# Products of a job under way go ahead of a due batch of values, and the second query block ends in two halves

## The chip, the core and the metric

The kernel runs on one core of a Trainium2 chip. The metric is device time in microseconds (us) of one execution. The kernel before was timed three times: 915.96, 916.36 and 916.58 us, median 916.36. A separate profiled execution took 916.05 us; its trace spans 914.0 us from the first to the last instruction.

## What is computed

A transformer layer with layer normalisation ahead of each part: attention with 32 heads of 20 columns over 2,048 rows of 640 columns, and then a gated product with 1,728 inner columns. Only the attention has an exponential; the gate is a plain product of two projections.

```
x = A_x                                            # 1 x 2048 x 640
qkv = layernorm(x) @ wqkv                          # 32 heads, 20 columns each
p = softmax(q @ k.T * 20 ** -0.5)                  # 2048 x 2048 for each head
h = x + (p @ v) @ wo
g = layernorm(h) @ w_gate;  u = layernorm(h) @ w_up
out = h + (g * u) @ w_down                         # 1728 inner columns
```

## The kernel before

**Blocks, groups, passes.** The 2,048 queries are cut into four blocks of 512 (b = 0 to 3), the 32 heads into eight groups of four. A pass handles one group with one block, against all 16 tiles of 128 keys. A pass named by a digit takes all 512 queries of its block; one named by a letter takes a half of 256 (`PASS`, lines 328 and 329): "C" and "D" are the halves of block 2, "A" and "B" those of block 3. Lines 330 to 339 write out the order of the passes. Blocks 0 and 1 run all eight groups in full; blocks 2 and 3 run `SPLIT_G` = 2 groups in full, then the other six for the first half and again for the second.

**Score tiles.** All passes together are cut into 683 score tiles of 1,536 columns (the last is shorter). For tile i, `emit_S` (line 519) puts the score products on PE (L533), which write one of two PSUM buffers `sc`; then ACT takes the exponential (L547) into one of six buffers `E`. In some tiles DVE takes the last 512 columns instead, by a polynomial in four steps (`emit_x`, lines 572 to 594: L580, L590, L591, L585); ACT's instruction is then 1,024 columns wide. Whether it does is decided by `x_takes` (line 566) for each tile: among its conditions, DVE must not be behind by the kernel's own bookkeeping, and in block 3 there must be `room()` (line 561), that is, the remaining tiles must leave room for the products of the tails that are still to be done.

**Values.** `emit_AV` (line 707) takes the finished exponentials in batches and multiplies them by the values (L740), accumulating in `acc`; a finished pass is copied out by DVE (L752) and divided by its sums. For most passes the division goes through DRAM: `norm` (line 629) sends the sums out and back (L636, L637), DVE takes reciprocals (L647), SP sends them to DRAM (L649) and back, spread over partitions (four transfers, L652), and DVE multiplies (L655). For the passes in `FAST` it is `job_norm` on PE.

**Jobs.** All other PE work is a queue of jobs: projections of q and k (L303), of values (L317), and the tail of each finished block, which is `job_out` (L978), normalisation, transposes (L283), the gate (`glu_sum` L1065 for 512 rows, `glu_two` L1083 for a half) and `job_y` (L1129, evacuated at L1133, stored by L1139). `run_job` (line 501) puts as many products of a job into each score tile's slot as fit by the bookkeeping `at` of expected times. Where nothing fits, `keep_warm` (L496) and line 529 put products with no use there. `due` (line 1306) lists the tails: a tail starts when its groups are normalised. The tails of blocks 0 and 1 take 512 rows, those of blocks 2 and 3 256. In the gate each of seven parts needs a pair of weight tiles (up and gate, 320 KB each), loaded by SP (L1036) into two buffers each. A program order by hand puts the spills of q to DRAM (L935, L936) behind block 0's tail. When the first tile of block 3 is reached, `load_res` puts four pairs for good into the buffers `qa`.

**The main loop** (lines 1310 to 1340) does this for each tile: scores and exponential; up to two batches of values; due events; a new tail if one is due; a job (`run_job`); fillers.

**The end.** After the last tile, `last_tail` (line 1218) does the last half of block 3 alone. It computes `out` for two row tiles (L1230, L1234), statistics on DVE, the scaled rows (DVE L1257, ACT L1258), then runs what is left in the queue of jobs (`fill`, line 1259), then transposes (lines 1260 and 1261), the gate (L1065) and `job_y`. What `fill` finds is `job_y` of the half before ("A"): one of its four pieces is held back for it by `add_tail` (lines 1190 to 1193), the others are there if they were not reached earlier.

Of the kernel before, what the change touches and what calls it, by code (L numbers as in the profile page):

```python
# [21 lines left out]
D = 640  # L22
H = 32
DH = 20
NT = S // P
# [3 lines left out]
HPG = 4  # L29
NG = H // HPG  # L30
VS = DH + 1
VW = H * VS + (SLOT - VS) + 1
QB = 512
# [6 lines left out]
FP = 7  # L40
FPW = 256
G1 = 4
SPLIT_G = 2
QA = 3 * QB
RES0 = 3
SM_SCALE = float(DH) ** -0.5
# [15 lines left out]
WO_NS, SUMS_NS, ROOT_NS, ROWS_NS = 1500, 6000, 5000, 5000  # L62
END_OF_TIME = 10 ** 9
WARM_LATE, NEXT_DVE = 0, 300
HOLD_AT, HOLD_NS = 5300, 450
AV_ROUNDS, X_LATE = 2, 0
FULL_IN, FULL_NS, ALL_NS = 2083, 300, 760
# [18 lines left out]
def kernel(  # L86
# [193 lines left out]
    def job_T(ln, dst, eng="dve", ps=None, after=None):  # L280
        ps = bank(BF16, D) if ps is None else ps
        for c in range(KT):
            nc.tensor.transpose(ps[:, c * P:(c + 1) * P], ln[:, c * P:(c + 1) * P], ident[:])  # L283
# [30 lines left out]
    def job_V(t, half):  # L314
        ps = bank()
        for c in range(KT):
# [9 lines left out]


    PASS = {"0": (0, 0, QB), "1": (1, 0, QB), "2": (2, 0, QB), "3": (3, 0, QB),
            "C": (2, 0, HW), "D": (2, HW, HW), "A": (3, 0, HW), "B": (3, HW, HW)}
    segs = []  # L330
    for ch in range(NB):
        for g in range(G1):
            kind = "copy" if ch == 0 else "last" if ch == NB - 1 else "add"
            segs.append(("0", g, ch * TPB, (ch + 1) * TPB, kind))
    segs += [("0", g, 0, NT, "only") for g in range(G1, NG)]
    segs += [("1", g, 0, NT, "only") for g in range(NG)]
    for full, halves in ("2", "CD"), ("3", "AB"):
        segs += [(full, g, 0, NT, "only") for g in range(SPLIT_G)]
        segs += [(p, g, 0, NT, "only") for p in halves for g in range(SPLIT_G, NG)]
    FINAL = len(segs) - 1  # L340
    TAILS = {0: [0], 1: [0], 2: [0, 2]}
    FAST = {("C", NG - 1), ("D", NG - 1), ("A", NG - 1), ("B", NG - 2)}

    tiles, cur_t, pos = [], [], 0
    for s, (p, g, lo, hi, _) in enumerate(segs):
# [358 lines left out]

    final = {}

    def emit_AV(upto):
        put_x()
        if not av_q:
# [274 lines left out]
            yield NEXT  # L984

    ln2 = {"open": 0, "rows": 0}
    COLUMNS_OF = {(1, 0): (0, 0), (1, 2): (0, 0), (2, 0): (1, 0), (2, 2): (1, 0), (3, 0): (2, 0)}

    def ln2_pieces(st, ts, key):
        while ln2["open"] >= 2 and not now["forced"]:  # L990
# [157 lines left out]
    LAST_B, LAST_T = NB - 1, [2, 3]  # L1148

    rows_in = set()  # L1150
    HELD_BY = {(1, 0): [(0, 0)], (2, 0): [(0, 2)], (2, 2): [(1, 0)], (3, 0): [(1, 2)]}

    def rows(b, ts):
        if b not in tail_st:
# [4 lines left out]

    def rows_early(b, ts):  # L1160
        key = b, ts[0]
        if key in HELD_BY and key not in rows_in and all(("y",) + k in done for k in HELD_BY[key]):
            rows(b, ts)

    def add_tail(b, ts):
# [48 lines left out]
    def run(gen):  # L1214
        for _ in gen:
            pass

    def last_tail():
# [36 lines left out]
        for hf in range(2):  # L1255
            cs = slice(hf * HALF, (hf + 1) * HALF)
            nc.vector.tensor_scalar(ls[ta][:, cs], ps_h[ta, hf][:, 0:HALF], m32[:, 0:1], r[:, 0:1], ALU.subtract, ALU.mult)  # L1257
            nc.scalar.activation(ls[tb][:, cs], ps_h[tb, hf][:, 0:HALF], ACT.Identity, bias=mr[:, 1:2], scale=r[:, 1:2])  # L1258
# [16 lines left out]
    def fill():  # L1275
        while step() is not None:
            pass
# [23 lines left out]
    def normed(p, gs):  # L1301
# [1 line left out]

    n_tiles = len(tiles)
    first_last = next(k for k, (us, _) in enumerate(tiles) if PASS[segs[us[0][0]][0]][0] == LAST_B)
    due = [("0", range(NG), 0, [0, 1, 2, 3]), ("1", range(NG), 1, [0, 1, 2, 3]), ("C", range(SPLIT_G, NG), 2, [0, 1]),
           ("D", range(SPLIT_G, NG), 2, [2, 3]), ("A", range(SPLIT_G, NG), 3, [0, 1])]
    PARTS = [d[2:] for d in due]
    i = 0
    while i < n_tiles or av_q:  # L1310
        now["i"] = i
        if i < n_tiles:
            emit_S(i)
        else:
            while step_x():
                pass
        if i == first_last:
            for g in range(NG):
                ensure(("spill", g))
            load_res()  # L1320
        if i == n_tiles:
            root = small.tile([P, 1], BF16, name="root")
            nc.scalar.activation(root[:], ones[:], ACT.Sqrt)
        for _ in range(2):
            emit_AV(i if i >= n_tiles else i - 2 if i >= LAG else i - 3)
            if not av_q or min(u[0] for u in av_q) > i - E_BUFS + 1:
                break
        run_events(i)
        if due:
            rows_early(*due[0][2:])  # L1330
        while due and normed(*due[0][0:2]) and (len(due[0][1]) == NG or normed(str(due[0][2]), range(SPLIT_G))):
# [112 lines left out]
```

## Time and profile before

| what | us |
|---|---|
| three timed runs | 915.96, 916.36, 916.58 |
| the profiled execution's own time | 916.05 |
| its span | 914.0 |
| ACT busy | 866.2 |
| PE busy | 817.5 |
| DVE busy | 702.1 |
| first exponential starts, last one ends | 15.6, 869.9 |

How to read it: each engine runs its own list of instructions in order, and semaphores hold one back until others are done. A row "x515 | 717.2, 1520 | 5.7" has the count, the time in which at least one of the group ran, the mean duration of one in ns (neighbours overlap), and the idle time of the engine ahead of them, with what ended it behind an arrow. In a timeline each row has its start and length. Rows of stretches have, for each engine, busy time and the count, then the granted clock of PE, the busy share of the DMA engines and GB/s.

### The profile page before, as it was taken

What the parts mean: (1) busy time and instruction counts of PE and PEld (TensorE: products, weight loads), DVE (VectorE), ACT (ScalarE), POOL (GpSimd) and SP (SyncE); (2) the same over time, 40 slices, a digit from 0 to 9 for tenths busy, and PEclk for the clock granted to TensorE, in tenths of its full rate; (3) what the DMA queues carried; (4) which work ended last, traced back from release to release, by engine and by line L of the source; (5) the groups of instructions that cost most, each with busy time, mean ns of one, the idle gap of its engine ahead of it and who ended that gap; (6) DMA issues with size and microseconds to landing.
All of it is one profiled execution on the core that took longest, in us unless ns stands there. A gap on an engine that the chain in (4) does not pass through costs nothing.

```text
span 914.0 us, 20094 instructions
## 1 busy us (share of the span) xinstructions
PE 817.5 (89%) x8035; PEld 346.8 (38%) x8115; DVE 702.1 (77%) x1310; ACT 866.2 (95%) x719; POOL 57.4 (6%) x255
## 2 busy tenths in 40 slices
PE   8788999889989899899897888999998999998897
PEld 5233333222223222233232333434434445444575
DVE  8664349899999899899998999798998784542243
ACT  6999999999999999999999999999999999999931
POOL 4210000000001200000003000020001000010000
PEclk9999999999999999999999999999999999999999
DMA  6000011011025022212410022021411211201310
GB/s 195 17 14 1 1 27 27 14 24 37 4 61 149 13 71 72 64 49 90 160 28 14 20 70 68 19 54 49 117 51 42 73 28 51 57 15 50 80 44 18
DMA packets 74203, 46.54 MB, mean 51 GB/s; under 512 B 20380, under 2 KB 70440, under 8 KB 74104
## 3 DMA queue, kind: packets, MB, share of 16 engines
q1 hardware_dynamic: 74104, 45.20, 18.0%
q8 instruction: 65, 1.06, 0.5%
q14 instruction: 34, 0.28, 0.1%
HBM read 37.88 MB, written 7.30 MB: 49 GB/s over the span
## 4 chain that ended last, share of the span: by engine, by line
ACT 67%; issue 17%; PE 10%; DVE 4%; DMA 1%; POOL 1%; SPq 0%; ACTq 0%
ACT E L547 67%; PE sc L533 2%; PE f L1065 2%; PE f L1129 2%; PE acc L740 1%; DVE st L201 1%; PE mi L303 1%; PE mi L978 0%; PE f L1230 0%; PE mi L496 0%; DMA wu<-in_B_w_up_dram 0%; PE mi L317 0%; PE mi L1083 0%; DVE kT L310 0%; DVE vx L270 0%
## 5 line engine op out<-in xcount | busy, mean ns | idle before, releaser
L547 ACT ACTIVATE E<-sc 128x1536 bf16<-128x1536 f32 (+1 forms) x683 | 848.7, 1417 | 6.2 <-PE sc L533 5.9
L533 PE MATMUL sc<-qa,kT 32*128 32x512 bf16 (+1 forms) x1920 | 203.2, 340 | 28.6 <-ACT E L547 16.9
L533 PEld LDWEIGHTS <-kT 32*128 32x128 bf16 x2816 | 84.1, 91 | 244.6 <-issue 206.1
L740 PE MATMUL acc<-E,vx 128*32 128x256 bf16 (+1 forms) x2592 | 170.3, 326 | 1.7 <-DVE vx L270 1.2
L580 DVE TENSOR_SCALAR xv<-sc 128x512 f32<-128x512 f32 x167 | 115.0, 689 | 30.2 <-PE sc L533 26.5
L585 DVE SCALAR_TENSOR_TENSOR xe<-xt,xv 128x512 int16<-128x512 f32 x167 | 113.3, 682 | 1.0
L591 DVE SCALAR_TENSOR_TENSOR xt<-xt,xv 128x512 f32<-128x512 f32 x167 | 112.3, 681 | 0.5
L590 DVE SCALAR_TENSOR_TENSOR xt<-xv 128x512 f32<-128x512 uint16 x167 | 112.0, 683 | 0.3
L303 PE MATMUL mi<-lnT,wp 128*128 128x512 bf16 x279 | 83.3, 381 | 11.7 <-DVE qa L310 5.5
L740 PEld LDWEIGHTS <-vx 128*32 128x32 bf16 x2816 | 55.8, 95 | 66.4 <-issue 63.8
L533 PE MATMUL sc<-qb,kT 32*128 32x256 bf16 (+1 forms) x896 | 68.2, 288 | 8.1 <-ACT E L547 5.3
L1129 PE MATMUL mi<-wd,hh 128*128 128x320 bf16 x336 | 58.2, 301 | 1.6 <-DVE xr L1133 1.6
L740 PE MATMUL acc<-xe,vx 128*32 128x512 bf16 (+1 forms) x224 | 50.6, 332 | 0.0
L1129 PEld LDWEIGHTS <-hh 128*128 128x128 bf16 x448 | 38.7, 97 | 30.6 <-issue 18.7
L303 PEld LDWEIGHTS <-wp 128*128 128x128 bf16 x310 | 25.0, 97 | 55.9 <-issue 44.3
L310 DVE TENSOR_SCALAR kT<-mi,one_row 128x512 bf16<-128x512 f32 x30 | 22.5, 750 | 28.1 <-PE mi L303 24.7
L1065 PE MATMUL mi<-ln2T,wg 128*128 128x512 bf16 x128 | 38.0, 382 | 5.8 <-DVE u L270 5.2
L496 PE MATMUL mi<-kT,ident 128*128 128x512 bf16 x116 | 37.8, 386 | 5.5 <-DVE ln2T L270 1.0
L978 PE MATMUL mi<-wo,on 128*128 128x320 bf16 x224 | 40.5, 301 | 2.2 <-DVE xr L982 2.0
L1065 PE MATMUL mi<-ln2T,wu 128*128 128x512 bf16 x128 | 37.3, 382 | 4.3 <-DVE hh L1073 3.5
L1083 PE MATMUL mi<-ln2T,qa 128*128 128x256 bf16 x240 | 34.6, 274 | 4.1 <-DVE hh L1091 3.0
L207 POOL CAST mb<-mv 128x2 bf16<-128x2 f32 (+1 forms) x10 | 2.3, 231 | 528.6 <-DVE mv L202 410.9
(143 smaller groups left out, 645.0 us busy)
## 6 DMA issues: line engine op xcount, KB each, us to landing
wu<-in_B_w_up_dram SPq DMA_DIRECT2D x23, 320.0 KB
wg<-in_B_w_gate_dram SPq DMA_DIRECT2D x23, 320.0 KB
bc<-scr SPq DMA_DIRECT2D x80, 64.0 KB
qsp<-qa SPq DMA_DIRECT2D x8, 384.0 KB
xr<-in_A_x_dram SPq DMA_DIRECT2D x16, 160.0 KB
bc<-scr SPq DMA_DIRECT2D x76, 32.0 KB
out_dram<-xr SPq DMA_DIRECT2D x14, 160.0 KB
wd<-in_B_w_down_dram SPq DMA_DIRECT2D x13, 160.0 KB
```

The lines of the kernel that those rows point to most:

```text
L303: nc.tensor.matmul(ps[:], lhsT=wslice(m, g, c), rhs=lnT[:, c, ch * QB:(ch + 1) * QB], start=(c == 0), stop=(c == KT - 1))
L496: nc.tensor.matmul(ps[:], lhsT=ident[:], rhs=kT[0][:, 0:BANK], start=True, stop=True)
L533: nc.tensor.matmul(sc[:, o:o + w], lhsT=kT[g][SLOT * j:SLOT * (j + 1), kt * P:(kt + 1) * P], rhs=q_of(g, b, c0, w)[SLOT * j:SLOT * (j + 1) ...
L547: exps = nc.scalar.activation(e[:, 0:n_act], sc[:, 0:n_act], ACT.Exp, bias=EXP_BIAS, scale=SM_SCALE)
L580: took = nc.vector.tensor_scalar(v[:], ps, X_SCALE, X_BASE, ALU.mult, ALU.max)
L585: nc.vector.scalar_tensor_tensor(e[:], t[:], X_R, v[:], ALU.mult, ALU.add)
L590: lambda: nc.vector.scalar_tensor_tensor(t[:], u, X_P, u, ALU.add, ALU.mult),
L591: lambda: nc.vector.scalar_tensor_tensor(t[:], t[:], X_Q, u, ALU.add, ALU.mult),
L740: nc.tensor.matmul(acc["t"][SLOT * j:SLOT * (j + 1), 0:w], lhsT=vx[kt][:, VS * h:VS * h + SLOT], rhs=e, start=(acc["n"][j] == 0), stop=(ac ...
L978: nc.tensor.matmul(ps[:, 0:HALF], lhsT=on[g][:, t * P:(t + 1) * P], rhs=wo[g][:, cs], start=(g == 0), stop=(g == NG - 1))
L1065: nc.tensor.matmul(ps[:, 0:n], lhsT=st["w", fp][k][:, c, f_cols(fp, f2)], rhs=st["ln2T"][:, c, c0:c0 + n], start=(c == 0), stop=(c == KT - 1))
L1129: nc.tensor.matmul(ps[:, 0:HALF], lhsT=st["hh"][f // 2][:, f % 2, t * P:(t + 1) * P], rhs=late["Wd"][f][:, cs], start=(f == 0), stop=(f == ...
```

## The change

Four things are altered.

1. `SPLIT_G` becomes a number for each block: 4 for block 1, 2 for block 2, 1 for block 3. So block 1 too ends in two halves ("E", "F") for its last four groups, its tail comes in two tails of 256 rows, and block 3 has one full group instead of two. The tables that depend on it (`TAILS`, `FAST`, `COLUMNS_OF`, `HELD_BY`, `due`) follow.
2. `job_ahead` is called in the main loop ahead of the batches of values. If a batch is due (`av_ns` gives its expected time) and a job is in the middle of a piece, it puts products of that job ahead of the batch, as far as both fit.
3. `rows_early` waits until the buffers of the tails are open, and may then load rows of block 1 early too.
4. In `last_tail`, `fill` is followed by products with no use, so many that both last `LN_NS` = 3,300 ns together.

```diff
-SPLIT_G = 2
+SPLIT_G = {"1": 4, "2": 2, "3": 1}
...
+LN_NS = 3300
...
+            "E": (1, 0, HW), "F": (1, HW, HW), "C": (2, 0, HW), "D": (2, HW, HW), "A": (3, 0, HW), "B": (3, HW, HW)}
...
-    segs += [("1", g, 0, NT, "only") for g in range(NG)]
-    for full, halves in ("2", "CD"), ("3", "AB"):
-        segs += [(full, g, 0, NT, "only") for g in range(SPLIT_G)]
-        segs += [(p, g, 0, NT, "only") for p in halves for g in range(SPLIT_G, NG)]
+    for full, halves in ("1", "EF"), ("2", "CD"), ("3", "AB"):
+        segs += [(full, g, 0, NT, "only") for g in range(SPLIT_G[full])]
+        segs += [(p, g, 0, NT, "only") for p in halves for g in range(SPLIT_G[full], NG)]
...
-    TAILS = {0: [0], 1: [0], 2: [0, 2]}
-    FAST = {("C", NG - 1), ("D", NG - 1), ("A", NG - 1), ("B", NG - 2)}
+    TAILS = {0: [0], 1: [0, 2], 2: [0, 2]}
+    FAST = {("E", NG - 1), ("F", NG - 1), ("C", NG - 1), ("D", NG - 1), ("A", NG - 1), ("B", NG - 2)}
...
+    def av_ns(upto):
+        if not av_q or acc["seg"] not in (None, av_q[0][1]):
+            return 0
+        s = av_q[0][1]
+        if acc["seg"] is None and at["pe"] < at["acc"] and now["i"] < acc["from"] and min(u[0] for u in av_q) > now["i"] - E_BUFS:
+            return 0
+        w = PASS[segs[s][0]][2]
+        most, rows = AV_ROUNDS * QB // w, [0] * HPG
+        for u in av_q:
+            if u[0] > upto or u[1] != s:
+                break
+            rows[u[3]] = min(rows[u[3]] + 1, most)
+        left = acc["left"] if acc["seg"] == s else END_OF_TIME
+        if sum(rows) < min(most * HPG, left) and min(u[0] for u in av_q) > upto - E_BUFS + 3:
+            return 0
+        return SWITCH + -(-sum(rows) // HPG) * (w * 5 // 12 + 4)
+
+    def job_ahead(upto):
+        ns = av_ns(upto)
+        if not ns:
+            return
+        until = max(at["exp"] - S_EXP - MARGIN, at["slot"][-2]) - ns
+        if not cur["fresh"]:
+            run_job(until)
...
-    COLUMNS_OF = {(1, 0): (0, 0), (1, 2): (0, 0), (2, 0): (1, 0), (2, 2): (1, 0), (3, 0): (2, 0)}
+    COLUMNS_OF = {(1, 0): (0, 0), (1, 2): (0, 0), (2, 0): (1, 0), (2, 2): (1, 2), (3, 0): (2, 0)}
...
-    HELD_BY = {(1, 0): [(0, 0)], (2, 0): [(0, 2)], (2, 2): [(1, 0)], (3, 0): [(1, 2)]}
+    HELD_BY = {(1, 0): [], (1, 2): [(0, 0)], (2, 0): [(0, 2)], (2, 2): [(1, 0)], (3, 0): [(1, 2)]}
...
-        if key in HELD_BY and key not in rows_in and all(("y",) + k in done for k in HELD_BY[key]):
+        if key in HELD_BY and key not in rows_in and ("open",) in done and all(("y",) + k in done for k in HELD_BY[key]):
...
+        begun = at["pe"]
         fill()
+        warm_ps = bank()
+        for _ in range(int((LN_NS - (at["pe"] - begun)) / 216)):
+            nc.tensor.matmul(warm_ps[:], lhsT=ident[:], rhs=kT[0][:, 0:BANK], start=True, stop=True)
...
-    due = [("0", range(NG), 0, [0, 1, 2, 3]), ("1", range(NG), 1, [0, 1, 2, 3]), ("C", range(SPLIT_G, NG), 2, [0, 1]),
-           ("D", range(SPLIT_G, NG), 2, [2, 3]), ("A", range(SPLIT_G, NG), 3, [0, 1])]
+    due = [("0", range(NG), 0, [0, 1, 2, 3]), ("E", range(SPLIT_G["1"], NG), 1, [0, 1]), ("F", range(SPLIT_G["1"], NG), 1, [2, 3]), ("C", range(SPLIT_G["2"], NG), 2, [0, 1]),
+           ("D", range(SPLIT_G["2"], NG), 2, [2, 3]), ("A", range(SPLIT_G["3"], NG), 3, [0, 1])]
...
+        if LAG <= i < n_tiles:
+            job_ahead(i - 2)
         for _ in range(2):
             emit_AV(i if i >= n_tiles else i - 2 if i >= LAG else i - 3)
```

More of the change, by code (lines that the diff above doesn't have):

```diff
@@ L328 @@
     PASS = {"0": (0, 0, QB), "1": (1, 0, QB), "2": (2, 0, QB), "3": (3, 0, QB),
-            "C": (2, 0, HW), "D": (2, HW, HW), "A": (3, 0, HW), "B": (3, HW, HW)}
+            "E": (1, 0, HW), "F": (1, HW, HW), "C": (2, 0, HW), "D": (2, HW, HW), "A": (3, 0, HW), "B": (3, HW, HW)}
     segs = []
@@ L1330 @@
             rows_early(*due[0][2:])
-        while due and normed(*due[0][0:2]) and (len(due[0][1]) == NG or normed(str(due[0][2]), range(SPLIT_G))):
+        while due and normed(*due[0][0:2]) and (len(due[0][1]) == NG or normed(str(due[0][2]), range(SPLIT_G[str(due[0][2])]))):
             add_tail(*due.pop(0)[2:])
```

## The prediction

> **What bounds the kernel now.** I read the page first, its busy shares and slices.
>
> ```profile
> span 914.0 us, 20094 instructions
> PE 817.5 (89%) x8035; PEld 346.8 (38%) x8115; DVE 702.1 (77%) x1310; ACT 866.2 (95%) x719; POOL 57.4 (6%) x255
> ...
> DVE  8664349899999899899998999798998784542243
> ACT  6999999999999999999999999999999999999931
> ```
>
> ACT is full from the second slice until the last two. PE and DVE are high too, but DVE thins out in the last ten slices. Next the groups of instructions, shapes kept apart, and three stretches.
>
> ```profile
> L547 ACT ACTIVATE E<-sc 128x1536 bf16<-128x1536 f32 x515 | 717.2, 1520 | 5.7 <-PE sc L533 5.5
> L547 ACT ACTIVATE E<-sc 128x1024 bf16<-128x1024 f32 x168 | 178.2, 1100 | 0.5 <-PE sc L533 0.5
> L580 DVE TENSOR_SCALAR xv<-sc 128x512 f32<-128x512 f32 x167 | 115.0, 689 | 30.2 <-PE sc L533 26.5
> L585 DVE SCALAR_TENSOR_TENSOR xe<-xt,xv 128x512 int16<-128x512 f32 x167 | 113.3, 682 | 1.0
> L1083 PE MATMUL mi<-ln2T,wu 128*128 128x256 bf16 x90 | 11.9, 273 | 2.0 <-DMA wu<-in_B_w_up_dram 1.0 <-DVE hh L1091 0.8 <-DMA sums_all<-sums 0.2
> L496 PE MATMUL mi<-kT,ident 128*128 128x512 bf16 x116 | 37.8, 386 | 5.5 <-DVE ln2T L270 1.0 <-DVE hh L1091 0.7 <-DVE vx L270 0.6
> ```
> ```profile
> 100.00:760.00 660.00, 596.05 (x5682) 225.40 (x5739) 579.57 (x1019) 659.10 (x542) 33.75 (x115) 1.00 0.19 53
> 760.00:870.00 110.00, 99.96 (x1367) 54.82 (x1373) 42.13 (x87) 109.14 (x84) 3.60 (x19) 1.00 0.17 46
> 870.00:914.00 44.00, 37.71 (x313) 29.57 (x312) 17.44 (x51) 9.86 (x24) 0.00 (x0) 0.97 0.11 32
> ```
>
> Until 870 us the exponentials set the time: ACT stood idle ahead of them for 5.7 + 0.5 = 6.2 us in all. So before 870 there are two ways to gain: fewer columns for ACT, or fewer of those 6.2 us. After 870 comes a chain of 44 us on PE, ACT and DVE, which the exponentials no longer touch; it gains separately.
>
> **The exponentials.** The instruction lists of the two built programs have 683 each. Before, 168 are 1,024 wide, after it 178: DVE takes ten more pieces of 512 columns. By the mean durations one is worth 1520 - 1100 = 420 ns, so 4.2 us. By busy time over count it is 717.2/515 - 178.2/168 = 1.393 - 1.061 = 0.33 us, so 3.3 us, the other end. The mean durations compare like with like, so I take **-4.2**. All ten lie past tile 600, and 84 of the 683 run from 760 us on (the count of ACT in the second stretch), so this is after about 760. DVE needs four steps for each, about 0.69 us each by its rows: 27.4 us. From 760 to 870 it is idle for 110.00 - 42.13 = 67.9 us, which is the cover; without it the ten would cost up to 27.4 us of waiting. The count is in the program, whatever the chip does.
>
> **Block 1 in halves.** Five groups (four of block 1, one of block 3) go at 256 instead of 512 columns: 320 more score products and 320 more value products, each half as wide, so the columns that PE streams stay equal. Three more normalisations pass through SP and two through PE; 38 of the products with no use (L496) go, seven more stand at line 529. 38 at 0.39 us at most are 14.7 us of PE time that cover these and the 42 products of L1129 that move forward (below, 42 x 0.14 = 5.9 us). **0** for PE; DVE's extra small copies lie in the same 67.9 us. The rows of block 1 come by the same transfers, only earlier, and nothing waits behind them but SP.
>
> **Weights.** Split tails read their weights once for each half: nine more pairs over SP. Before, one pair came late where the profile shows it:
>
> ```profile
> 752.18 0.32 SPq L649 DMA_DIRECT2D scr<-ri  x1
> 753.59 2.60 SPq L652 DMA_DIRECT2D bc<-scr  x4
> 756.23 0.42 SPq L1036 DMA_DIRECT2D wu<-in_B_w_up_dram  x1
> ```
> ```profile
> 759.73 1.27 PE L1083 MATMUL mi<-ln2T,wu 128*128 128x256 bf16 x10 [1.03 <-DMA wu<-in_B_w_up_dram]
> ```
> ```profile
> 761.44 9.68 ACT L547 ACTIVATE E<-sc 128x1536 bf16<-128x1536 f32 x7 [0.84 <-PE sc L533]
> ```
>
> SP issued the pair only after a normalisation's five transfers, the first use stood two tiles on, PE waited 1.03 us and ACT 0.84. In the new lists that place is gone (the pair there has four tiles), but in block 1's first half a pair again stands behind one L649 and four L652, one tile ahead of its use. A tile is 660/542 = 1.22 us. So the change of this term lies between -0.84 (no stall), and +1.2 (the same stall, one tile longer); uncovered by any tile it would be about 3.5 us from the issue at 756.23 to 759.73, that is +2.7. I take **+0.2**, the middle of the nearer two.
>
> **Spills.** Behind block 0's tail stand 16 transfers of q.
>
> ```profile
> L936 SPq DMA_DIRECT2D qsp<-qb x8: 432/451/563, 432.1 to 441.9; - x8
> ```
> ```profile
> 440.00:445.00 5.00, 4.04 (x35) 1.20 (x34) 3.56 (x7) 5.00 (x5) 0.00 (x0) 1.00 0.83 317
> ```
> ```profile
> 527.06 1.62 SPq L1036 DMA_DIRECT2D wu<-in_B_w_up_dram  x1
> ```
>
> They kept the DMA engines busy until about 440 + 0.83 x 5 = 444.2 us, and the next weights came at 527. In the new lists weights for block 1's first half follow right behind the last spill, four tiles (4.9 us) ahead of their use. From the last spill's issue, about 442, to the drain are 2.2 us, and 3.5 for the landing make 5.7: 0.8 late. Bounds 0 and 1.6 (up and gate both late), taken **+0.4**.
>
> **Products ahead of values.** The gain is in a place like this one, where a key projection's last products stood behind a batch of values.
>
> ```profile
> 52.12 0.62 PE L740 MATMUL acc<-E,vx 128*32 128x512 bf16 x8
> 52.67 0.60 PE L303 MATMUL mi<-lnT,wp 128*128 128x512 bf16 x2
> 53.31 0.75 DVE L310 TENSOR_SCALAR kT<-mi,one_row 128x512 bf16<-128x512 f32 x1 [0.28 <-PE mi L303]
> 54.12 0.39 PE L533 MATMUL sc<-qa,kT 32*128 32x512 bf16 x1 [0.53 <-DVE kT L310]
> 54.60 4.13 ACT L547 ACTIVATE E<-sc 128x1536 bf16<-128x1536 f32 x3 [0.54 <-PE sc L533]
> ```
>
> With the two first, DVE's evacuation starts 52.67 - 52.12 = 0.55 us earlier, and ACT's 0.54 us of idling go: **-0.5**. The other early stalls have the same order in both lists. Behind the products waits only the batch, whose exponentials are two tiles old; its delay is hidden by the six buffers `E`, and a later release of one would be seen as ACT waiting for L740. Bounds -0.54 and 0.
>
> **The end.** Earlier tails mean that three of the four pieces of `job_y` which `fill` found are done before the last tile.
>
> ```profile
> 875.98 7.83 PE L1129 MATMUL f<-wd,hh 128*128 128x320 bf16 x56
> 883.65 0.44 PE L283 MATMUL mi<-ident,ln 128*128 128x128 bf16 x5
> 883.93 0.44 PE L283 MATMUL acc<-ident,ln 128*128 128x128 bf16 x5
> ```
> ```profile
> 878.28 1.12 DVE L1257 TENSOR_SCALAR ln<-f,m,rstd 128x320 bf16<-128x320 f32 x2
> 878.44 1.13 ACT L1258 ACTIVATE ln<-f,mr,rstd 128x320 bf16<-128x320 f32 x2 [0.48 <-DVE mr L1253]
> ```
>
> The scaled rows are ready at 878.44 + 1.13 = 879.57, but PE is still in 56 products until 883.65: 4.08 us for nothing. The new list has 14 there (7.83/56 = 0.14 each, so until 877.94) and six products with no use. At 0.6 - 0.39 = 0.21 us apart (the pair of L303 above, less one duration of L496) these end at 879.2, inside the wait; at 0.39 each they end at 880.3. So the transposes come 4.08 or 3.4 us earlier, and all behind them with it. **-4.0**.
>
> **The clock**, a rule that speaks against the change.
>
> ```profile
> 500.00:505.00 5.00, 3.23 (x59) 1.36 (x58) 4.47 (x8) 5.00 (x6) 3.71 (x12) 1.00 0.02 2
> 505.00:506.00 1.00, 1.00 (x14) 0.27 (x9) 1.00 (x4) 1.00 (x2) 0.00 (x0) 0.64 0.07 16
> 507.00:508.00 1.00, 1.00 (x18) 0.48 (x20) 0.96 (x3) 1.00 (x2) 0.00 (x0) 0.50 0.00 0
> ```
> ```profile
> 509.62 1.94 ACT L547 ACTIVATE E<-sc 128x1024 bf16<-128x1024 f32 x2 [0.49 <-PE sc L533]
> ```
>
> After a stretch in which PE was busy for 3.23 of 5 us its clock fell to 0.50, and ACT lost 0.49 us. With 38 products fewer to fill such stretches there may be none or three of them, -0.5 to +1.0 against now; I take 0, since the lists hold about as much PE work. The Trainium skill (TensorE: Matmul & The Clock Gate, Part 1: The HAM clock gate) has the clock halve after an idle window of about 3.4 us. The 0.50 agrees; the idle window does not, for PE was 65% busy here. By the rule the new kernel loses nothing to the clock as long as PE has no such window, and the sum would be 0.5 lower; by the row it stands as it is.
>
> **Sum.** -4.2 + 0.2 + 0.4 - 0.5 - 4.0 = -8.1 on the profiled execution's 916.05: 907.95. The three runs' median, 916.36, is 0.3 above that execution, within their own spread of 0.6; I forecast **908.0**.
>
> **Rivals.**
> - *More stalls in the middle*: weights late at two or three places and clock drops at three. For it: block 1's halves have no resident weights, as block 3 has. 2.7 + 1.6 - 0.6 already counted + 1.0 gives 912.7 at the most, 911 as its centre. 18%.
> - *The end keeps its length*: the transposes wait for something else, as a slower clock or a late DVE. Nothing between 879.57 and 883.65 but PE's own list holds them. 908.0 + 4.0 = 912.0. 7%.
> - *More gained*: the late weights and the clock drop vanish and nothing comes for them: 908.0 - 0.84 - 0.2 - 0.4 - 0.49 = 906.1, or less where smaller waits go too. 12%.
> - *Nothing comes of it*: the ten shorter exponentials are eaten by new waits on DVE, and the end stays. 916. 3%.
> - *Slower, by SP's order*: in block 1's halves each weight pair queues behind a normalisation, as at 752 to 756, and ACT waits 0.84 + 1.22 = 2.06 us for each. With nine: 916.05 - 8.7 + 18.5 = 925.9; from five late pairs on (8.7/2.06 = 4.2) it is slower than before. Against it: in the row of L1083 above, 1.0 us in all of waiting for up weights, over 90 products. 4%.
>
> **How the numbers follow.** The forecast has 56%. Its own bounds run from -4.2 - 0.84 - 0.54 - 4.08 - 0.5 (905.9) to the first rival's 912.7. The range of 905.2 to 912.4 takes in the two rivals on either side nearly whole and leaves out the last two and the edges. A measurement of this kernel can tell about 0.2% (1.8 us) from no change; faster, below 914.5: 93%, within: 3%, slower: 4%.
>
> **What would show it.** 178 exponentials of 1,024 columns and about 6 us of idle time ahead of L547. ACT's last exponential ending near 865.5. From the last exponential to the end of the span 40.1 instead of 44.1 us, with 14 products of L1129 ahead of the transposes. No idle at the place of 54.60. A stall of about a microsecond in block 1's halves, ended by weights. I am wrong if ACT's idle time grows past 10 us, or if the transposes begin later than 10 us after the last exponential.

## The result and the profile after

The changed kernel takes 925.61 us (median of four runs, 923.68 to 928.43) where the kernel before, on the same chip, takes 916.31 (915.96 to 916.58). The ratio is 1.0099, 95% interval 1.0081 to 1.0117: slower by about 9 us, where 8 us less were forecast. The profiled execution took 925.74 us.

The page of the changed kernel, busy shares and slices:

```profile
span 923.7 us, 21787 instructions
PE 826.3 (89%) x8821; PEld 370.0 (40%) x8886; DVE 730.6 (79%) x1369; ACT 864.5 (94%) x719; POOL 60.3 (7%) x255
...
DVE  8654349998997899899897889998799988964342
ACT  6989999999998999999998999999899999999951
```

ACT is busy for 1.7 us less than before in a span that is 9.7 us longer, and its row shows 8s in the middle where there were only 9s. The exponentials, shapes kept apart, and the waits that concern them (us in total, times, the longest):

```profile
L547 ACT ACTIVATE E<-sc 128x1536 bf16<-128x1536 f32 x505 | 703.3, 1501 | 13.3 <-PE sc L533 10.3 <-PE acc L765 2.4
L547 ACT ACTIVATE E<-sc 128x1024 bf16<-128x1024 f32 x178 | 185.1, 1071 | 7.8 <-PE sc L533 7.6
```
```profile
ACT E L547 <- PE sc L533: 17.9, 18, 3.2
...
DVE rstd L239 <- POOL den L233: 8.7, 5, 3.3
...
PEld L1108 <- DMA wu<-in_B_w_up_dram: 4.2, 3, 2.1
...
DVE ri L647 <- DMA sums_all<-sums: 3.5, 1, 3.5
...
ACT E L547 <- PE acc L765: 2.4, 4, 0.8
```

The 178 narrow exponentials are there. But ACT is idle ahead of L547 for 13.3 + 7.8 = 21.1 us, before 6.2. The last exponential ends at 883.5 (before 869.9), and the rest of the span takes 40.2 us (before 44.1). Followed back from each idle stretch of ACT to what was late, the 21.1 us fall into these parts:

| what was late | ACT idle, us | at |
|---|---|---|
| POOL's square root of a tail's normalisation | 0.89 + 1.50 + 1.03 + 0.56 + 0.83 = 4.8 | 313, 493, 497, 824, 829 |
| weights behind a normalisation on SP | 1.64 + 1.54 + 1.05 = 4.2 | 526, 661, 665 |
| sums of a pass behind loads on SP | 3.20 + 0.38 = 3.6 | 283, 286 |
| a buffer `E`, held by a late batch of values | 2.4 | 330, 382, 409, 766 |
| the first 60 us, and small ones | 6.1 | before too, 4.9 |

Each place needs one look. **The sums.** SP's own queue, in the kernel before and in the changed one:

```profile
266.81 0.50 SPq L636 DMA_DIRECT2D sums<-asb  x1
268.50 0.34 SPq L637 DMA_DIRECT2D sums_all<-sums  x1
268.94 1.80 SPq L965 DMA_DIRECT2D xr<-in_A_x_dram  x4
...
273.35 9.22 SPq L956 DMA_DIRECT2D wd<-in_B_w_down_dram  x14
```
```profile
265.77 8.09 SPq L981 DMA_DIRECT2D wd<-in_B_w_down_dram  x14
273.91 1.06 SPq L990 DMA_DIRECT2D xr<-in_A_x_dram  x2
275.07 0.51 SPq L636 DMA_DIRECT2D sums<-asb  x1
```

Before, a pass's sums went out and back ahead of the tail's loads. In the changed kernel the 14 loads of `wd` are reached first and take SP 8.09 us to issue; the sums leave at 275.07. What follows, all engines:

```profile
279.83 0.25 DVE L647 RECIPROCAL ri<-sums_all 128x16 f32<-128x16 f32 x1 [3.50 <-DMA sums_all<-sums]
...
281.07 1.55 PE L1003 MATMUL mi<-wo,on 128*128 128x320 bf16 x8 [2.89 <-DVE xr L1007]
...
283.27 2.37 ACT L547 ACTIVATE E<-sc 128x1024 bf16<-128x1024 f32 x2 [3.20 <-PE sc L533]
```

DVE runs its list in order, so it stands at the reciprocal for 3.50 us. Its evacuation at L1007 stands behind that, PE waits 2.89 us for the evacuation, the next scores stand behind PE's wait, and ACT loses 3.20.

**The weights.** All engines again, around 655 us:

```profile
654.97 0.88 SPq L652 DMA_DIRECT2D bc<-scr  x2
655.90 0.42 SPq L1061 DMA_DIRECT2D wu<-in_B_w_up_dram  x1
...
659.29 0.94 PE L1108 MATMUL mi<-ln2T,wu 128*128 128x256 bf16 x7 [1.83 <-DVE xe L585]
...
660.68 1.45 ACT L547 ACTIVATE E<-sc 128x1536 bf16<-128x1536 f32 x1 [1.54 <-PE sc L533]
```

The pair leaves SP behind the transfers of L652 (the last two of four are shown), and PE's product is 3.4 us behind its issue. The page names DVE as the releaser, which ended in the same instant; the wait of PE's weight load (2.1 us, the longest in its row above) shows that the data was not there either. This cause is read from SP's list; no run below moves these loads alone.

**POOL.** The statistics of a tail go to POOL for 19 small steps (L208 to L233; one lower in the kernel before), and the planner puts DVE's reciprocal (L239) into DVE's list `ROOT_NS` = 5,000 ns later by its own bookkeeping. First a chain of the kernel before and the reciprocal that waits for it, then the last chain after:

```profile
477.81 0.18 POOL L207 CAST mb<-mv 128x2 bf16<-128x2 f32 x1 [172.61 <-DVE mv L202]
...
485.23 0.20 POOL L232 TENSOR_TENSOR den<-v,y 128x2 bf16<-128x2 f32 x1
```
```profile
485.46 0.17 DVE L238 RECIPROCAL rstd<-den 128x2 f32<-128x2 bf16 x1 [1.07 <-POOL den L232]
```
```profile
814.85 0.53 POOL L208 CAST mb<-mv 128x2 bf16<-128x2 f32 x1 [111.08 <-DVE mv L203]
...
818.22 0.65 POOL L222 TENSOR_TENSOR nt<-y 128x2 f32<-128x2 f32 x1
818.94 0.20 POOL L224 TENSOR_TENSOR nt<-nt,v 128x2 f32<-128x2 f32 x1
...
821.97 0.20 POOL L233 TENSOR_TENSOR den<-v,y 128x2 bf16<-128x2 f32 x1
```
```profile
818.12 0.69 DVE L585 SCALAR_TENSOR_TENSOR xe<-xt,xv 128x512 int16<-128x512 f32 x1
818.73 0.20 DVE L647 RECIPROCAL ri<-sums_all 128x8 f32<-128x8 f32 x1
822.20 0.17 DVE L239 RECIPROCAL rstd<-den 128x2 f32<-128x2 bf16 x1 [3.28 <-POOL den L233]
```

The last chain after took 7.32 us. While DVE works through the polynomial, six of its first seven steps take 0.5 to 0.66 us; from 818.94 on, with DVE idle, a step takes 0.19 to 0.20. DVE reached its reciprocal early, stood there for 3.28 us, and ACT lost 0.56 behind it.

But POOL was about as slow before. The chain shown took 7.62 us; of the seven chains behind the first 60 us, those of the kernel before took 4.96 to 7.70 us (6.6 in the mean), those of the changed kernel 6.18 to 8.07 (7.0). What differs is how soon DVE is free for the reciprocal. Before, it waited in two chains, free 6.6 and 6.8 us after their start, for 1.07 and 0.91 us, and ACT lost nothing over 0.25 us behind them. After, it waited in five, free 4.1 to 6.3 us after their start, for 0.92 to 3.28 us, and behind three of them ACT lost the 4.8 us of the table.

**The clock.** Stretches of 3.4 us, each followed by the next one; the first number after the length is PE's busy time, and the third from the end the granted clock:

```profile
46.36:49.77 3.41, 2.49 (x19) 0.99 (x22) 1.33 (x3) 2.28 (x3) 0.00 (x0) 1.00 0.27 100
49.77:53.18 3.41, 3.37 (x18) 1.05 (x11) 1.81 (x4) 2.67 (x3) 0.00 (x0) 0.50 0.02 5
278.50:281.90 3.40, 0.82 (x7) 0.59 (x7) 2.07 (x5) 1.57 (x2) 0.00 (x0) 1.00 0.05 5
281.90:285.30 3.40, 3.40 (x22) 0.84 (x19) 2.87 (x6) 2.03 (x2) 0.00 (x0) 0.50 0.27 77
...
657.35:660.76 3.41, 1.58 (x21) 0.94 (x16) 1.94 (x4) 1.87 (x3) 0.00 (x0) 1.00 0.67 182
660.76:664.17 3.41, 3.18 (x24) 1.51 (x21) 1.98 (x3) 2.71 (x2) 0.00 (x0) 0.50 0.69 184
```

A wait of PE is paid twice: after a stretch with too little work the clock is 0.50 for 3.41 us. That happens five times ahead of the last exponential (50, 282, 494, 661, 825 us), before once. The losses at 497, 665 and 829 in the table (2.9 us) lie at the end of such stretches or, at 829, right behind one.

### The profile page after: what moved, and what is told of

Read it like the earlier page. It is cut to its first block, busy times and chain, and to the rows that moved or that the text cites. A ratio compares the mean times of both kernels' runs of the same rounds, so it can differ in the third digit from the quotient of the medians.

```text
span 923.7 us, 21787 instructions
## 1 busy us (share of the span) xinstructions
PE 826.3 (89%) x8821; PEld 370.0 (40%) x8886; DVE 730.6 (79%) x1369; ACT 864.5 (94%) x719; POOL 60.3 (7%) x255
## 4 chain that ended last, share of the span: by engine, by line
ACT 48%; PE 26%; issue 13%; DVE 9%; POOL 2%; DMA 1%; SPq 0%; ACTq 0%; DVEq 0%
ACT E L547 48%; PE sc L533 6%; PE acc L765 4%; PE mi L1108 4%; PE mi L1090 2%; PE f L1090 2%; PE mi L1154 1%; PE mi L1003 1%; DVE xv L580 1%; DVE st L202 1%; PE f L1154 1%; PE mi L496 1%; DVE u L1113 1%; PE mi L304 1%; DVE xt L591 1%
## 5 line engine op out<-in xcount | busy, mean ns | idle before, releaser
L547 ACT ACTIVATE E<-sc 128x1536 bf16<-128x1536 f32 (+1 forms) x683 | 847.1, 1389 | 21.1 <-PE sc L533 17.9
L533 PE MATMUL sc<-qa,kT 32*128 32x256 bf16 (+1 forms) x2176 | 204.9, 320 | 23.2 <-ACT E L547 14.0
L765 PE MATMUL acc<-E,vx 128*32 128x256 bf16 (+1 forms) x2855 | 172.5, 312 | 2.2 <-DVE vx L271 1.2
L580 DVE TENSOR_SCALAR xv<-sc 128x512 f32<-128x512 f32 x177 | 121.9, 689 | 37.2 <-PE sc L533 34.9
L585 DVE SCALAR_TENSOR_TENSOR xe<-xt,xv 128x512 int16<-128x512 f32 x177 | 119.7, 681 | 0.8
L591 DVE SCALAR_TENSOR_TENSOR xt<-xt,xv 128x512 f32<-128x512 f32 x177 | 119.0, 680 | 0.7
L590 DVE SCALAR_TENSOR_TENSOR xt<-xv 128x512 f32<-128x512 uint16 x177 | 118.3, 681 | 0.3
L765 PEld LDWEIGHTS <-vx 128*32 128x32 bf16 x3136 | 66.3, 96 | 71.1 <-issue 67.7
L1154 PE MATMUL mi<-wd,hh 128*128 128x320 bf16 x378 | 65.9, 301 | 1.6 <-DVE xr L1158 1.6
L765 PE MATMUL acc<-xe,vx 128*32 128x256 bf16 (+1 forms) x281 | 56.0, 307 | 0.0
L1108 PE MATMUL mi<-ln2T,wg 128*128 128x256 bf16 x250 | 37.8, 279 | 4.9 <-DVE u L1113 4.8
L1108 PE MATMUL mi<-ln2T,wu 128*128 128x256 bf16 x250 | 36.0, 275 | 5.9 <-DVE hh L1116 2.0
L208 POOL CAST mb<-mv 128x2 bf16<-128x2 f32 (+1 forms) x10 | 2.9, 292 | 539.0 <-DVE mv L203 539.0
L1113 DVE CAST u<-mi 128x512 bf16<-128x512 f32 x35 | 24.0, 687 | 13.5 <-PE mi L1108 13.0
L318 PE MATMUL mi<-wv,lnT 128*128 128x320 bf16 x160 | 29.1, 305 | 4.6 <-DVE vx L271 2.6
```

Source lines behind the costliest of these rows:

```text
L533: nc.tensor.matmul(sc[:, o:o + w], lhsT=kT[g][SLOT * j:SLOT * (j + 1), kt * P:(kt + 1) * P], rhs=q_of(g, b, c0, w)[SLOT * j:SLOT * (j + 1) ...
L547: exps = nc.scalar.activation(e[:, 0:n_act], sc[:, 0:n_act], ACT.Exp, bias=EXP_BIAS, scale=SM_SCALE)
L580: took = nc.vector.tensor_scalar(v[:], ps, X_SCALE, X_BASE, ALU.mult, ALU.max)
L585: nc.vector.scalar_tensor_tensor(e[:], t[:], X_R, v[:], ALU.mult, ALU.add)
L590: lambda: nc.vector.scalar_tensor_tensor(t[:], u, X_P, u, ALU.add, ALU.mult),
L591: lambda: nc.vector.scalar_tensor_tensor(t[:], t[:], X_Q, u, ALU.add, ALU.mult),
```

## The experiments

The parts of the loss can be taken away one at a time. In each run below, "ACT idle" is the idle time ahead of L547 in its profiled execution, to be held against 21.1 (after) and 6.2 (before).

**e2_wd_late: the loads of `wd` later.** The changed kernel, with

```diff
-                load_wd()
+                later(14, load_wd)
```

> The changed kernel, with the 14 transfers of w_down put 14 tiles later, so that they no longer stand ahead of the sums of a pass on SP. Theory S: the stall at 283 us (3.4 + 0.5 us of ACT) goes and with it one clock drop: about 921.7, DVE's wait for sums_all 0. Theory P: that stall goes too, but the four stalls behind POOL stay, 921 to 922, with ACT idle 17. If the halves themselves overload PE: 925.6.

Measured: 920.22 us, ratio 1.0032 [1.0018, 1.0046]. ACT idle 14.2; the wait of L647 for the sums is gone from the list of waits, the waits for POOL are not (8.8 us). SP's queue now reads:

```profile
267.04 0.51 SPq L636 DMA_DIRECT2D sums<-asb  x1
...
278.64 6.71 SPq L981 DMA_DIRECT2D wd<-in_B_w_down_dram  x14
```

The lists of ACT and POOL are the same as in the changed kernel, and DVE's differs in 25 places, so this run changes hardly anything but SP's order, and that order was the cause of the 3.6 us at 283. The ratio falls by 0.0067, some 6 us. That is more than the 3.6, and more than the 921 to 922 us and the idle time of 17 that were expected: the profile has two half-clock stretches ahead of the last exponential in place of five.

**e1_root9: the reciprocal later.** The changed kernel, with

```diff
-WO_NS, SUMS_NS, ROOT_NS, ROWS_NS = 1500, 6000, 5000, 5000
+WO_NS, SUMS_NS, ROOT_NS, ROWS_NS = 1500, 6000, 9000, 5000
```

> The changed kernel, with 9,000 instead of 5,000 ns allowed for POOL's Newton steps (ROOT_NS) before DVE's reciprocal is put in its list. Theory P (POOL's 19 steps take 6.2 to 8.1 us beside DVE's polynomial steps, DVE then waits at the reciprocal, PE behind it, and the clock drops): DVE's waiting for POOL falls from 8.7 to under 1 us, ACT's idle time from 21.1 to about 14, clock drops from 5 to 2 or fewer; 175 instead of 178 narrow exponentials cost 1.3 back: about 918.5. Theory S (SP's queue is the cause of most) and theory V (values pushed back by job_ahead): within 1.5 us of 925.6.

Measured: 921.33 us over eight runs, 1.0032 [1.0009, 1.0056]. The waits for POOL fall from 8.7 to 3.3 us, not to under 1. The one that is left is the last chain's: DVE is free 4.07 us after its start with 9,000 ns as with 5,000, so `ROOT_NS` does not set it; here ACT loses nothing over 0.25 us behind it. The wait for the sums stays, and it is longer (4.87 us of ACT at 281). The rest of the expectation missed too. The profiled execution, the slowest of the eight (925.41), has 17.7 us of idle time where about 14 were expected, and ahead of the last exponential four half-clock stretches of 6.8 us each. DVE's list differs from that of the changed kernel from 29 us on, and the order has 175 narrow exponentials, so the edit changes more than the place of the reciprocals.

**e5_root9_wd: both edits.**

> Both edits together. P and S together: 925.6 - 7.4 - 3.6 + 1.3 = 916 or a little lower, since with both gone few clock drops are left. If the causes are others that only move (a stall goes, the next in line comes): above 920.

Measured: 916.71 us, 0.9994 [0.9981, 1.0007]. ACT idle 8.0. The two edits together take away the whole loss, and the kernel is where it was before the change. Against e1 it again changes hardly anything but SP's order (ACT's and POOL's lists are the same, DVE's differs in 25 places), so the 0.0038 between the two, 3.5 us, is a second measure of what that order costs. With 175 narrow exponentials (7 x 0.42 = 2.9 us) and an end of 40.9 us (3.2) it should be 6 us ahead. Its profiled execution is ahead by 2.2 (913.89 against 916.05), with 8.0 - 6.2 = 1.8 us more of idle time and about as much by exponentials that start later behind a stall; its other runs have a lower clock than that one (0.994 in the mean, 0.997 there; the price is given at the end).

**e7_no_poly_block3: no polynomial in block 3.** Is it DVE's polynomial that slows POOL? In the changed kernel, ACT takes all of block 3's pieces:

```diff
-        return (n == EW and segs[s][4] == "only" and (PASS[segs[s][0]][0] < LAST_B or room()) and last_tile[s] - i >= X_LEAST
+        return (n == EW and segs[s][4] == "only" and PASS[segs[s][0]][0] < LAST_B and last_tile[s] - i >= X_LEAST
```

> The changed kernel with DVE's polynomial never used in block 3: 135 narrow exponentials instead of 178, so 18.4 us more for ACT, about 942 if nothing else moves. It is there for POOL's steps at about 815 us and later. Theory P, with DVE's steps from SBUF to SBUF as what slows POOL: POOL's 19 steps of the last half take about 5.0 us, as in the kernel before (4.96, DVE 10% busy), not 7.3, and DVE does not wait for them. If something else slows POOL (transfers, the halves): still above 6.5 us.

Measured, one execution: 940.79 us, since 43 exponentials more are wide. POOL's last two chains took 4.96 us each (6.74 and 7.32 in the changed kernel); the earlier ones, still beside the polynomial, were as slow as in the changed kernel. The same step of the last chain:

```profile
816.17 0.19 POOL L222 TENSOR_TENSOR nt<-y 128x2 f32<-128x2 f32 x1
...
819.47 0.20 POOL L233 TENSOR_TENSOR den<-v,y 128x2 bf16<-128x2 f32 x1
```

0.19 us instead of 0.65, with nothing else changed in the chain. So the polynomial is what slows POOL's steps. The other half of the expectation, that DVE would not wait, missed:

```profile
819.70 0.17 DVE L239 RECIPROCAL rstd<-den 128x2 f32<-128x2 bf16 x1 [4.74 <-POOL den L233]
```

With less work of its own, DVE stands at the reciprocal 0.25 us after the chain's start and waits 4.74 us for a chain of 4.96. No idle time of ACT over 0.25 us follows. The length of the wait is therefore not a measure of how slow POOL is, nor of what ACT loses.

**e4_ahead_only: products ahead of values alone.** The kernel before, with `av_ns`, `job_ahead` and its call.

> The kernel before with job_ahead alone; block 1 whole, as before. 175 instead of 168 narrow exponentials: 7 x 0.427 = 3.0 us less for ACT. If putting products ahead of values is harmless, 913 to 914.5. Theory V (a batch of values behind a job's products comes too late, and ACT waits for a buffer E): ACT idle behind L740 of 2 us and more, 916 or higher. If theory P holds here too, what decides is whether DVE waits for POOL's steps: its total at the reciprocal, 2.0 us before.

Measured: 918.99 us, 1.0019 [1.0002, 1.0036]. 175 narrow exponentials, so most of the -4.2 comes with this part. ACT idle 12.9: the wait for the sums is here too (2.43 us of ACT at 282), POOL's waits are 6.2 us, the waits for values 1.2.

**ah_wd: the same with `wd` later.**

> The kernel before with the products ahead of values alone, and its last weights of a batch asked for later, as in the repaired changed kernel. If the wait for the sums at 282 us (2.4 us) in the run without this edit came from SP's order, it is gone, and the time is 915 to 917.5 us (918.99 less some 2 to 4); the POOL waits (6.2 us there) should stay within 4 to 8. If the sums were late for another reason, the wait stays and the time stays at 918 to 920.

Measured: 915.32 us, 0.9984 [0.9972, 0.9997]. No wait for the sums is left, and ACT runs through the place; POOL's waits stay at 6.2 us:

```profile
274.86 14.62 ACT L547 ACTIVATE E<-sc 128x1536 bf16<-128x1536 f32 x12
```
```profile
DVE rstd L238 <- POOL den L232: 6.2, 4, 3.4
...
ACT E L547 <- PE acc L765: 1.3, 2, 0.7
```

So the wait for the sums comes with products ahead of values, not with block 1's halves, through the order in which SP's list is written. Against e4 the lists of ACT and POOL are the same; the ratio is 0.0035 lower, a third measure of that order.

**e6_halves_only: the halves and the end, without products ahead.** The changed kernel, without the call, and with the hold on block 1's rows restored in part:

```diff
-    HELD_BY = {(1, 0): [], (1, 2): [(0, 0)], (2, 0): [(0, 2)], (2, 2): [(1, 0)], (3, 0): [(1, 2)]}
+    HELD_BY = {(1, 0): [(0, 0)], (1, 2): [(0, 0)], (2, 0): [(0, 2)], (2, 2): [(1, 0)], (3, 0): [(1, 2)]}
...
-            job_ahead(i - 2)
+            pass
```

> The changed kernel without job_ahead, and with the rows of block 1's first half loaded only after block 0's first half of y. Blocks in halves, one full group in block 3 and the products of last_tail stay. 166 narrow exponentials, 2 fewer than before: +0.9 us; 14 products of L1129 ahead of the transposes: -4.0. In its list the sums of no pass stand behind the transfers of w_down. If job_ahead is what brings most of the stalls (it opens block 0's tail earlier, in front of a pass's sums, and pushes values back): 913 to 914.5, ACT idle about 7, ACT's waiting behind L765 none. If the halves bring them (SP's weights, POOL's steps): 920 or more, with DVE waiting 5 us and more for POOL.

Measured: 920.1 us (916.32 to 925.17), 1.0037 [1.0018, 1.0056]; ACT idle 7.5, of it 1.35 us at 534 from late weights; 166 narrow exponentials and 41.5 us for the end. A miss: the time lies where it was expected if the halves bring the stalls, the waits (2.6 us for POOL, 0.7 for values) where it was expected if the products ahead bring them. It is not the products ahead alone that cost, and the halves alone do not gain. The profiled execution took 917.15 us, of which 916.05 + 0.9 - 2.6 + 1.3 = 915.7 is accounted for (two wide exponentials more, the end, the idle time); the median is 3 us above it, at a mean clock of 0.995 against 0.999. What else costs here is not shown.

Side by side, for before, products ahead alone, halves alone, and both: DVE's waits for POOL are 2.0, 6.2, 2.6 and 8.7 us; its waits for the sums 0, 3.0, 0.2 and 3.5; the waits of PE's weight loads for up weights in the halves' gate (L1083 before, L1108 in the others) 1.3, 0, 2.5 and 4.2. So the sums and most of POOL's waits come with the products ahead, the late weights with the halves. The two parts' losses, 0.0019 and 0.0037, do not add up to 0.0099; each kernel has an order of its own.

**e8_root7_wd and e9_root7_margin: a version that gains.** Both have `wd` later and `ROOT_NS` = 7000; e9 also gives the products ahead less room:

```diff
-        until = max(at["exp"] - S_EXP - MARGIN, at["slot"][-2]) - ns
+        until = max(at["exp"] - S_EXP - MARGIN, at["slot"][-2]) - ns - 150
```

> The changed kernel with 7,000 ns for POOL's steps and the transfers of w_down 14 tiles later; 174 narrow exponentials. Theory P: most of POOL's chains end within 7.3 us, so this is as good as 9,000 (916.7), within 1.5 us. If only the wider allowance counts, it keeps a wait for POOL of 3 to 5 us and lies at 918 to 920.

> As the one with 7,000 ns, and job_ahead stops 150 ns earlier. If values pushed back by job_ahead are what ACT waits for behind L765 (2.3 to 2.6 us in the runs so far): this falls to about 1 us and the time by 1 to 1.5. If not, the same time within 0.5 us and the same waits.

Measured: e8 919.37 us, 1.0022 [1.0007, 1.0038], with a stall of 4.17 us at 651 for late weights and 4.2 us of DVE's waits for POOL, as was expected if only the wider allowance counts. e9 912.12 us (911.01 to 914.45), **0.9948 [0.9931, 0.9966]**, faster than both kernels. The exponentials and the waits of e9:

```profile
L547 ACT ACTIVATE E<-sc 128x1536 bf16<-128x1536 f32 (+1 forms) x683 | 847.0, 1400 | 9.4 <-PE acc L765 4.6 <-PE sc L533 4.1 <-ACT E L547 0.4
```
```profile
DVE ri L647 <- DMA sums_all<-sums: 1.1, 1, 1.1
DVE rstd L239 <- POOL den L233: 1.0, 1, 1.0
```

The reason given for its third edit fell: waits for values were to become fewer and grew from 2.4 (after) and 4.0 (e8) to 4.6 us. Its order happens to be one without the stall of e8 at 651, and its runs have a mean clock of 0.998.

**Other draws of the order.** Most edits let the planner draw another order. How far does that alone move the time? `NEXT_DVE`, a constant of the planner that decides where spare products go, was moved from 300 to 280 or 320.

> The changed kernel with one planner constant moved, NEXT_DVE 300 to 280, which re-rolls the order of products and exponentials (176 narrow ones in place of 178) without touching what is computed or any of the four kinds of stall on purpose. If the loss is the change's own (waits that it brings in systematically), this stays at 921 to 928 us with ACT idle near 18 to 22 us and POOL waits of 5 us or more. If the order was an unlucky draw, such a draw moves the time by several us either way: 914 to 921, with other places for the stalls. If before's time was itself a lucky draw, the two perturbed befores are slower than 918.

> The changed kernel with NEXT_DVE 300 to 320 (178 narrow exponentials). If the loss is systematic, 921 to 928 us, ACT idle near 18 to 22 us. If it is a draw of the order, another value between 914 and 928, differing from the sister kernel by more than 3 us.

> The kernel before with NEXT_DVE 300 to 280 (166 narrow exponentials, so 0.9 us more or less of base sum). If before is an ordinary draw of its planner, 915 to 918.5 us, ACT idle 5 to 9 us. If before is a lucky draw, 918.5 to 924 us with ACT idle of 10 us or more, from the same kinds of wait (POOL, the sums, weights, values).

> The kernel before with NEXT_DVE 300 to 320 (169 narrow exponentials). If before is an ordinary draw, 915 to 918.5 us, ACT idle 5 to 9 us; if a lucky one, 918.5 to 924 us and ACT idle of 10 us or more.

> The fastest variant so far (weight loads four tiles later, ROOT_NS 7000, products ahead given 150 ns less room; 912.1 us) with NEXT_DVE 280 in place of 300, a redraw of its order. If the gain comes from its three edits it keeps 909 to 914.5 us, POOL waits of 2 us or less and no wait for the sums. If 912.1 was the draw, it returns to 916 to 921 us, where the same kernel without the last edit stands (919.4).

| kernel | `NEXT_DVE` | us | ratio | ACT idle |
|---|---|---|---|---|
| a_n280, changed | 280 | 928.71 | 1.0133 [1.0116, 1.0150] | 23.0 |
| a_n320, changed | 320 | 925.94 | 1.0107 [1.0090, 1.0124] | 18.5 |
| b_n280, before | 280 | 923.90 | 1.0080 [1.0063, 1.0097] | 12.1 |
| b_n320, before | 320 | 917.63 | 1.0016 [1.0002, 1.0030] | 5.6 |
| m_n280, e9 | 280 | 912.77 | 0.9954 [0.9936, 0.9972] | 8.8 |

At 320 the changed kernel's instruction lists came out the same as at 300 but for four places on DVE and two on PE, so a_n320 repeats it rather than redraws it. m_n280 differs from e9 in six places on DVE, so it too is nearly a repetition. (In e9, and so in m_n280, it is the 14 loads of `wd` that come later, by 14 tiles.) a_n280 has the same lists as the changed kernel for the first 577 us on every engine, and another order only behind that. That it has the same stalls up to 526 therefore says nothing; behind 577 it has again a wait for late weights (ACT loses 3.81 us at 660) and one for POOL (0.58 at 828). The redraws of before have other orders from 235 us (280) and 428 us (320) on. And before is not a settled value: one redraw lands near where it was, the other 7.5 us higher, mostly by a POOL wait:

```profile
309.26 0.17 DVE L238 RECIPROCAL rstd<-den 128x2 f32<-128x2 bf16 x1 [3.93 <-POOL den L232]
...
312.82 1.45 ACT L547 ACTIVATE E<-sc 128x1536 bf16<-128x1536 f32 x1 [3.44 <-PE sc L533]
```

This chain ran at full speed, 5.00 us from 304.23; DVE was free 1.10 us after its start, and ACT lost 3.44.

What stays open: how much of the loss of 9 us belongs to the change, and how much to the good order in which before happens to stand. The sums' place on SP is shown as a cause by three pairs of runs. The weights behind a normalisation are read from the lists. For POOL the waits are shown, and that later reciprocals take most of them away; why the planner's list brings DVE to the reciprocals so early is not. No run draws another order for the first 577 us of the changed kernel without a repair, so it is not shown that such an order could not avoid the stalls, and e9 avoids most. Whether e9's 912.1 is its edits or a good draw is open in the same way, since m_n280 hardly tests it.

## Why the prediction was wrong

The profiled execution went from 916.05 to 925.74, by +9.7 us, where -8.1 was the sum. Term by term:

- **The exponentials, -4.2: right in the count.** 178 narrow ones, and the ten more lie past tile 600. No row shows the 4.2 us by itself: ACT's busy time fell by 1.7, for which see below.
- **The end, -4.0: right.** 40.2 us from the last exponential, forecast 40.1. The list of PE after the last exponential shows the 14 products, and the transposes behind them 9.3 us after it (13.7 before):

```profile
889.57 2.06 PE L1154 MATMUL f<-wd,hh 128*128 128x320 bf16 x14
891.47 1.46 PE L1288 MATMUL f<-kT,ident 128*128 128x512 bf16 x5
892.76 0.62 PE L284 MATMUL mi<-ident,ln 128*128 128x128 bf16 x5
```

- **Spills, +0.4: nothing.** The last spill leaves SP at 502, and no idle time of ACT over 0.25 us lies between 498 and 523.
- **Products ahead, -0.5: right in its place, and yet the step that failed first.** With nearly the same list in a_n320, ACT ran eight exponentials through the place of 54.60:

```profile
47.30 11.08 ACT L547 ACTIVATE E<-sc 128x1536 bf16<-128x1536 f32 x8 [1.13 <-PE sc L533]
```

  The profiled execution of the changed kernel stalled there for 0.74 and 0.31 us, because its clock was 0.50 from 49.8 on. What failed is the cost: "Behind the products waits only the batch" and "its delay is hidden by the six buffers `E`". The products ahead also open block 0's tail earlier: in e4 its first weights leave SP at 262.7, before at 270.9. So 14 loads of `wd` come ahead of a pass's sums on SP, the reciprocal that waits for the sums stops DVE, PE and ACT in turn, and 3.6 us go. e2, e5 against e1, and ah_wd show it. And ACT waited 2.4 us for L765, in the sign that the prediction itself had named; the halves alone have 0.7 of that, so not all of it need be the products'.
- **Block 1 in halves, 0: too low.** Its "nothing waits behind them but SP" looked at the rows of block 1; what came late behind other transfers were the weights of the next item. The halves alone (e6) stand at 920.1 us.
- **Weights, +0.2: mis-sized.** The stall of before at 761 went (-0.84), and two pairs came late (526 and 661), for 4.2 us with the half-clock stretch behind the second: +3.4 net. The place in the list that I had found, in block 1's first half, was the one at 526; the other lies in block 2's first half. The rival by SP's order had 2.06 us for each late pair. The two stalls themselves are 1.64 and 1.54 us; that 4.2/2 = 2.1 comes so near is luck, since it holds 1.05 us of slow clock, which the price had not.
- **The clock, 0: wrong.** Five half-clock stretches for one, where up to three were allowed for. Four more at 1.1 us, the estimate worked out at the end, are some 4 us, in part the same idle time.
- **A term was missing: POOL.** The sum has no line on the 19 steps of POOL, although before's trace has chains of 7.2 to 7.7 us for an allowance of 5.0, and 2.0 us of waits for L238. It took for granted that each reciprocal keeps its place against its chain. It did not: DVE is free for it 4.1 to 6.3 us after the chain's start where it waits, and 4.8 us of ACT's idle time follow. The waits come mostly with the products ahead (6.2 us in e4). The Trainium skill (SBUF — State Buffer, Who interferes with whom) has a DVE instruction with two SBUF inputs contend with a GpSimd instruction that reads SBUF, so that the later one blocks; the trace agrees, 0.5 to 0.66 us beside L591 and L585 against 0.19 alone.

Together: -4.2 - 3.9 in the two terms that held, and +14.9 of idle time (21.1 - 6.2), a good part of it behind waits that the planner places by expected times. The first exponential starts 0.4 later. The remaining 2.5 us are most likely overlap that was lost: neighbours overlap, in the row at 824 us below by 1.50 - (4.21 - 1.50)/2 = 0.15 us, and an exponential behind a stall has no neighbour to overlap with. With 22 waits for PE in place of 9 that is, as an estimate, 2.0 us.

```profile
824.02 4.21 ACT L547 ACTIVATE E<-sc 128x1536 bf16<-128x1536 f32 x3 [0.56 <-PE sc L533]
```

Of the rivals, "slower, by SP's order" was nearest: right in sign and, by luck, in size (925.9). Only half of the idle time that was added is SP's (4.2 + 3.6 of 14.9), and it had taken nine late pairs where there were two. Of the two signs of being wrong that were set beforehand, the idle time past 10 us came (21.1), late transposes did not.

## What to carry to other kernels

When a change moves work in a schedule, list every wait that is put into an engine's list by an expected time (here a root on POOL, sums through DRAM, weights), and ask for each whether its slack survives: when the waiter arrives, as well as how long the work takes. A count of instructions on the busiest engine says nothing of that. On a queue shared by loads and small urgent transfers, look at what comes to stand behind the loads as well as at the loads. Before a tuned schedule is taken as the base of a comparison, redraw its order once or twice: here that alone moved the time by up to 7.5 us, nearly as much as the change.

## What the runs showed of the hardware

- **The clock falls without an idle stretch.** The drops in one execution lie at whole multiples of 3.413 us from one another (in the profile after 68, 130, 179 and 227 of them from the first), so the stretches that decide lie on a fixed grid, and a stall can fall into one or be split between two. In the 3.41 us ahead of a drop in that profile, PE was busy for 24% to 73% of the time (0.82 and 2.49 us in the rows above). Over all 16 profiles, between the first and the last exponential, each of the 16 stretches with PE busy for under half was followed by one at half clock, and 16 of the 144 between a half and three quarters; above that it was rare (11 of 3,865). The Trainium skill (TensorE: Matmul & The Clock Gate, What's actually happening) has such free-running windows of 3,413 ns, which agrees, and names an idle window as what halves the clock, which does not: no window ahead of the five drops was idle.
- **What a drop costs.** Among runs of one and the same program, the time falls by 0.58 us for each 0.001 of the mean granted clock (101 runs of 14 programs, deviations from each program's mean; correlation -0.92). One half-clock stretch lowers the mean by 3.41 x 0.5/918 = 0.0019, so by this line it goes with about 1.1 us, an estimate that holds part of the stall which brought it. The runs of the changed kernel have a mean of 0.990, the runs of before on the chips of the experiments some 0.996: about 3.5 of the 9 us by the same estimate.
- **POOL beside DVE.** The same step takes 0.19 us alone and 0.5 to 0.66 beside the polynomial's later steps, which are 0.68 to 0.69 us long. Which step runs decides: in the profiles before and after, 54 of the 55 POOL steps that began beside L590, L591 or L585, whose inputs all lie in SBUF, took over 0.3 us, and none of the 44 beside L580, which reads PSUM, took more than 0.22. A busy DVE alone does not do it: the chain at 22 us took 5.03 us with DVE 85% busy with other work, ahead of the polynomial; with DVE 92% busy, most of it polynomial, the chain at 434 us took 8.07.
